# A fused chunked-attention and gated feed-forward kernel: SP's DMA queue in program order, 112-row first loads, feed-forward units moved ahead of an out-projection, masks by matmul

## The chip, the cores and the metric

The kernel runs on one core of one Trainium2 chip. The metric is the time of one execution on the device in microseconds (us). A *profile* is one execution recorded by the hardware profiler; its span runs from the first to the last recorded instruction and is about 1.7 us shorter than the time of the same execution (277.73 and 276.0 before); an execution's time also varies by a few us around the medians quoted. Engines are called as the profile calls them: PE (matmuls), PEld (its weight loads), DVE (vector), ACT (scalar), POOL (general), SP (here it only issues DMAs); "SPq" is SP's instruction queue. Each engine has one queue of instructions, and in these profiles one that waits holds up those behind it (below, a cast on DVE that waits 3.88 us). A scheduler decides the order of each queue when the kernel is built, from its own guess of durations. `keep_in_program_order` pins an instruction behind the one that the program writes before it for the same engine; where that one is not pinned and moves ahead, the pinned one can follow it (`e9_b2_after_wout` shows a case).

## The reference

Four batches of 768 tokens, 8 heads of 64. A chunk of 32 queries sees 16 keys to its left, itself, 8 keys to its right, and 8 memory keys. The result, 3072 tokens of 512 features, goes through a gated feed-forward layer.

```python
for c in range(nc):                                   # 24 chunks of 32
    k_full = concat([mem_k, k[:, :, max(0, 32*c-16) : min(S, 32*c+40)]])
    v_full = ...                                      # the same of v
    a = softmax(q_c @ k_full.T / 8)
    out[:, :, 32*c : 32*c+32] = a @ v_full
x = out.transpose(0, 2, 1, 3).reshape(3072, 512)
y = (relu(x @ w_gate) * (x @ w_val)) @ w_out          # 512 -> 1536 -> 512
```

## The kernel before

It works in 8 blocks of 384 tokens (half a batch). A block's feed-forward is 12 *dff units* (each four gate matmuls and four value matmuls of 128x384, then a product on DVE) and an *out-projection* (36 matmuls of 128x512, three stores). The attention of block n+1 is woven between the dff units of block n, so that in the long run PE never stops. I call "block n" the stage from the end of block n-1's out-projection to the end of its own.

Blocks 0 and 1 must be quick to start: four tokens per partition, so 100 partitions for 400 keys, and transposes on PE. The later blocks are loaded one token per partition, and keys, queries and attention output are transposed by DMAs issued from SP. SP thus issues three kinds of DMA in one queue: loads, transposes, and stores.

```python
KROWS = 100
def sp(dst, src):   return pin(nc.sync.dma_start(dst, src))      # pin = keep_in_program_order
def pool(dst, src): return pin(nc.gpsimd.dma_start(dst, src))

# start (cut): block 0 on SP and ACT, then weights on POOL, then block 1, then the rest
for h0 in (0, 4):
    b0.load_kv("k", h0, 4, sp); b0.load_q(h0, 4, act); b0.load_kv("v", h0, 4, sp)
# POOL waits until block 0's second keys are here, then loads w_gate, w_val columns 0 to 511
weights(0, 256); weights(256, 512)
sp(w_here[:, 0:1], w_val_sb[0:1, 0, 0:1])        # SP waits for the first weights
for h0 in (0, 4): ...                            # block 1's k, q, v, all on SP
# POOL waits until block 1's second keys are here, then
weights(512, 1024); weights(1024, 1536)
for c in range(0, NDC, 4): pool(w_out_sb[:, c:c + 4], ...)

# main loop (cut): ffn = 12 dff units, then the 3 units of the out-projection
    if n == 0:
        def first_load(b2=b2):
            sp(w_here[:, 1:2], w_out_sb[0:1, NDC - 1, 0:1])   # SP waits for w_out
            b2.load(sp)
        steps[11] = [first_load]
    elif n + 2 < NBLK:
        steps[0] = [lambda b2=b2: b2.load(nc.sync.dma_start)]   # not pinned
    ...                                          # steps 8 to 14: casts and transposes of block n+2

    def turn_k(self): nc.sync.dma_start_transpose(self.kT..., self.kn...)      # not pinned
    def turn_q(self): nc.sync.dma_start_transpose(self.qT..., self.qn...)      # not pinned
    def cast_q(self): ... nc.vector.tensor_copy(self.qn..., view...)
    def cast_v(self): nc.vector.tensor_copy(self.vb[:, :, :, 0:D], self.vf); ...
```

The softmax here doesn't subtract the row's maximum and nothing guards it: scores larger than these inputs give would overflow.

## Time and profile before

281.69 us (median of 2 runs, 281.11 to 282.26). The profiled span is 276.0 us. The page's head gives busy time by engine, and rows of 40 slices of 6.9 us each in tenths; PEclk is the granted PE clock, DMA the mean busy share of the 16 DMA engines.

```profile
span 276.0 us, 4450 instructions
PE 235.2 (85%) x1592; PEld 136.2 (49%) x1592; DVE 154.2 (56%) x399; ACT 112.1 (41%) x229; POOL 32.8 (12%) x60
PE   0386756994999989989989997959999999999994
PEclk9999595999799999999999999986999999999999
DMA  6698899959799798984997799398601121111001
```

The next view cuts the span into stretches: length, busy time of each engine (with the number of instructions), mean clock, DMA share, GB/s. The cuts are at the first gate matmul (29.6), the end of block 1's out-projection (108.0), and the ends of blocks 2 to 5.

```profile
0.00:29.60 29.60, 12.80 (x125) 9.65 (x126) 17.66 (x57) 15.53 (x33) 15.46 (x45) 0.97 0.79 170
29.60:108.00 78.40, 66.06 (x436) 37.33 (x436) 43.07 (x112) 30.56 (x65) 9.78 (x11) 0.90 0.97 188
108.00:135.10 27.10, 25.94 (x182) 15.19 (x181) 18.65 (x46) 11.56 (x23) 1.88 (x1) 1.00 0.91 193
135.10:162.80 27.70, 26.31 (x182) 15.02 (x181) 19.31 (x48) 11.56 (x23) 1.88 (x1) 1.00 0.90 176
162.80:197.10 34.30, 29.16 (x182) 15.78 (x181) 21.61 (x50) 11.56 (x23) 3.77 (x2) 0.90 0.91 185
197.10:222.80 25.70, 25.70 (x182) 15.24 (x181) 14.16 (x38) 11.56 (x23) 0.00 (x0) 1.00 0.16 48
```

Block 5 (the last row) has PE busy in all of its 25.7 us, and that is what a block costs when nothing disturbs it. Blocks 2, 3 and 4 take 27.1, 27.7 and 34.3: 12.0 us more than three such blocks. The first two blocks take 108.0 us.

The load of block 7's queries (178.29) stands behind a transpose of attention output, which can go only when that attention is done. It landed at 184.8. On DVE a cast of those queries stands in order between products that PE needs, and waits for them:

```profile
184.78 0.56 DVE L257 CAST qn_106<-qf 128x768 bf16<-128x768 f32 x1 [3.88 <-DMA qf<-in_q_dram]
```

On PE this is seen:

```profile
185.86 1.44 PE L360 MATMUL vl_ps<-xT,w_val_sb 128*128 128x384 f16 x4 [3.24 <-DVE gvT L365]
187.10 10.14 PE L375 MATMUL out_ps<-w_out_sb,gvT 128*128 128x512 f16 x36
```

PE waited 3.24 us, then ran at half its clock for a few microseconds: four value matmuls in 1.44 us (0.81 elsewhere), an out-projection in 10.14 (7.93 elsewhere).

### The profile page before, as it was taken

The numbers are of one execution on the slowest core, as the hardware profiler recorded it, in microseconds if no ns is written. First come the engines' busy times: TensorE is split into PE (matmuls) and PEld (weight loads), VectorE is DVE, ScalarE is ACT, GpSimd is POOL, SyncE is SP. The second block draws the span as 40 slices with busy tenths as digits, with TensorE's granted clock in tenths as the row PEclk, the third lists the DMA queues.
The fourth block names the chain that finished last, engine by engine and source line by source line (L and its number), as shares of the span: only waits on it lengthen the run. The fifth ranks groups of instructions, "written<-read, shape, count | busy, mean of one in ns | idle before, by whom it ended". The sixth has DMA issues, their size and how long they took to land.

```text
span 276.0 us, 4450 instructions
## 1 busy us (share of the span) xinstructions
PE 235.2 (85%) x1592; PEld 136.2 (49%) x1592; DVE 154.2 (56%) x399; ACT 112.1 (41%) x229; POOL 32.8 (12%) x60
## 2 busy tenths in 40 slices
PE   0386756994999989989989997959999999999994
PEld 0264322653455645655546554633566466645641
DVE  5566131586527973896289619944687138703410
ACT  1575522554435523642345234520365246414321
POOL 8490250000020200020020002000200000000000
PEclk9999595999799999999999999986999999999999
DMA  6698899959799798984997799398601121111001
GB/s 163 185 131 184 216 206 196 197 88 255 121 210 252 117 201 263 194 174 96 274 201 152 163 208 252 62 211 150 173 14 32 52 77 23 37 76 40 0 38 77
DMA packets 96506, 39.76 MB, mean 144 GB/s; under 512 B 76324, under 2 KB 93412, under 8 KB 96484
## 3 DMA queue, kind: packets, MB, share of 16 engines
q1 hardware_dynamic: 89620, 33.97, 56.9%
q0 software_dynamic: 5808, 4.72, 11.0%
q10 hardware_dynamic: 1056, 0.79, 1.0%
q8 instruction: 12, 0.20, 0.3%
q14 instruction: 10, 0.08, 0.1%
HBM read 30.03 MB, written 6.29 MB: 132 GB/s over the span
## 4 chain that ended last, share of the span: by engine, by line
PE 55%; DMA 20%; DVE 10%; issue 6%; POOL 4%; SPq 2%; ACT 1%; DVEq 0%; POOLq 0%; ACTq 0%
PE out_ps L375 23%; PE vl_ps L360 14%; PE g_ps L356 14%; DMA w_out_sb<-in_moe_w_out_dram 8%; DMA qf<-in_q_dram 4%; DVE gvT L365 4%; DMA kf_100<-in_k_dram 3%; DVE x_big L313 2%; DMA w_val_sb<-in_moe_w_val_dram 2%; PE s_ps L294 2%; DMA kf_99<-in_k_dram 2%; SPq L387 2%; DVE ex_111 L302 1%; PE o_ps L308 1%; POOL w_gate_sb L390 1%
## 5 line engine op out<-in xcount | busy, mean ns | idle before, releaser
L360 PE MATMUL vl_ps<-xT,w_val_sb 128*128 128x384 f16 x384 | 82.2, 337 | 6.6 <-DVE gvT L365 4.1
L356 PE MATMUL g_ps<-xT,w_gate_sb 128*128 128x384 f16 x384 | 81.8, 335 | 4.9 <-DMA w_gate_sb<-in_moe_w_gate_dram 3.4
L365 DVE TENSOR_TENSOR gvT<-vl_ps,g_relu 128x384 f16<-128x384 f32 x96 | 52.9, 552 | 56.3 <-PE vl_ps L360 55.4
L363 ACT ACTIVATE g_relu<-g_ps 128x384 f16<-128x384 f32 x96 | 47.1, 490 | 52.9 <-PE g_ps L356 38.4
L375 PE MATMUL out_ps<-w_out_sb,gvT 128*128 128x512 f16 x288 | 65.8, 388 | 0.0
L360 PEld LDWEIGHTS <-w_val_sb 128*128 128x128 f16 x384 | 38.3, 100 | 33.9 <-issue 8.3
L356 PEld LDWEIGHTS <-w_gate_sb 128*128 128x128 f16 x384 | 36.6, 100 | 24.0 <-issue 3.9
L375 PEld LDWEIGHTS <-gvT 128*128 128x128 f16 x288 | 28.7, 100 | 34.9 <-issue 3.3
L378 ACT COPY o_sb<-out_ps 128x512 f32<-128x512 f32 x24 | 14.0, 585 | 59.4 <-PE out_ps L375 59.4
L313 DVE TENSOR_TENSOR x_big<-o_ps,rinv 96x256 f16<-96x256 f32 x64 | 26.5, 414 | 0.8
L299 ACT ACTIVATE ex_110<-s_ps 128x384 f16<-128x384 f32 x22 | 10.9, 493 | 12.8 <-PE s_ps L294 8.8
L294 PE MATMUL s_ps<-qz_97,kb 128*128 128x192 bf16 x64 | 11.0, 257 | 3.9 <-DVE qz_97 L212 3.6
L294 PEld LDWEIGHTS <-kb 128*128 128x128 bf16 x128 | 10.2, 99 | 6.9 <-issue 3.9
L299 ACT ACTIVATE ex_112<-s_ps 128x384 f16<-128x384 f32 x21 | 10.3, 492 | 7.4 <-PE s_ps L294 5.7
L299 ACT ACTIVATE ex_111<-s_ps 128x384 f16<-128x384 f32 x21 | 10.3, 492 | 7.3 <-PE s_ps L294 6.9
L311 DVE RECIPROCAL rinv<-o_ps 96x4 f32<-96x4 f32 x64 | 10.8, 168 | 2.1 <-PE o_ps L308 2.0
L294 PE MATMUL s_ps<-qz_98,kb 128*128 128x192 bf16 x64 | 11.0, 244 | 0.0
L302 DVE TENSOR_TENSOR ex_111<-ex_111,mask_int 128x384 f16<-128x384 f16 x16 | 10.1, 630 | 0.2
L308 PEld LDWEIGHTS <-ex_111 128*128 128x128 f16 x84 | 5.0, 100 | 10.1 <-DVE ex_111 L302 6.6
L257 DVE CAST qn_106<-qf 128x768 bf16<-128x768 f32 x6 | 3.2, 551 | 11.0 <-DMA qf<-in_q_dram 11.0
L267 POOL CAST vb_108<-memv 8x2048 f16<-8x2048 f32 x2 | 3.8, 1883 | 44.8 <-DVE vb_108 L264 44.8
L267 POOL CAST vb_107<-memv 8x2048 f16<-8x2048 f32 x2 | 3.9, 1950 | 40.0 <-DVE vb_107 L264 40.0
(114 smaller groups left out, 184.4 us busy)
## 6 DMA issues: line engine op xcount, KB each, us to landing
out_dram<-o_sb SPq DMA_DIRECT2D x24, 256.0 KB
qf<-in_q_dram SPq DMA_DIRECT2D x6, 768.0 KB
vf_102<-in_v_dram SPq DMA_DIRECT2D x12, 240.0 KB
vf_101<-in_v_dram SPq DMA_DIRECT2D x12, 240.0 KB
kf_100<-in_k_dram SPq DMA_DIRECT2D x9, 256.0 KB
kf_99<-in_k_dram SPq DMA_DIRECT2D x9, 256.0 KB
w_out_sb<-in_moe_w_out_dram POOLq DMA_DIRECT2D x3, 512.0 KB, 20.4
w_gate_sb<-in_moe_w_gate_dram POOLq DMA_DIRECT2D x2, 512.0 KB, 10.3
```

Source lines behind the costliest of these rows:

```text
L294: nc.tensor.matmul(s_ps[:, i], lhsT=blk.kb[:, 2 * g + i, j, :], rhs=blk.qz[:, 2 * g + i, :, :, 32 * j:32 * j + 32], start=True, stop=True)
L299: nc.scalar.activation(e, s_ps.rearrange("p a x s c -> p (a x) (s c)"), ACT.Exp, scale=SCALE)
L302: nc.vector.tensor_tensor(out=e, in0=e, in1=m4, op=ALU.mult)
L308: nc.tensor.matmul(o_ps[:, i, :], lhsT=st["ex"][:, i, :], rhs=blk.vb[:, j, 4 * g + i, :], start=True, stop=True)
L311: nc.vector.reciprocal(rinv, o_ps[0:QB, :, D:D + 1])
L313: nc.vector.tensor_tensor(out=x_big[:, 256 * g:256 * g + 256].rearrange("p (h d) -> p h d", h=4), in0=o_ps[0:QB, :, 0:D], in1=rinv_b, op=A ...
L356: nc.tensor.matmul(g_ps, lhsT=w_gate_sb[:, f, 128 * m:128 * m + 128], rhs=blk.xT[:, f, :], start=(f == 0), stop=(f == NFC - 1))
L360: nc.tensor.matmul(vl_ps, lhsT=w_val_sb[:, f, 128 * m:128 * m + 128], rhs=blk.xT[:, f, :], start=(f == 0), stop=(f == NFC - 1))
L363: nc.scalar.activation(g_relu, g_ps, ACT.Relu)
L365: nc.vector.tensor_tensor(out=state["gvT"][:, m].rearrange("p t j c -> p j t c"), in0=vl_ps.rearrange("p (j t c) -> p j t c", j=NJ, t=NT), ...
L375: nc.tensor.matmul(out_ps, lhsT=state["gvT"][:, m, t].rearrange("p j c -> p (j c)"), rhs=w_out_sb[:, m, :], start=(m == 0), stop=(m == NDC ...
L378: nc.scalar.copy(o_sb, out_ps)
```

## The change

Its intents: SP's whole queue is pinned, so that loads go before the stores and transposes that follow them in the program; loads are given in the order of need, and each block's preparation is moved up; the first two blocks are loaded in 112 rows (of four tokens, so 448 tokens instead of 400), to use more DMA engines; block 1's dff units come before block 0's out-projection, so that `w_out` is needed later; the masks of blocks 0 and 1 are added to the scores by a small matmul instead of a product on DVE; in the later blocks the cast of q goes to ACT, that of v to POOL; and idle matmuls are put in at the start to keep the PE clock up. The core of the diff (the rest is renaming, the two halves of start attention handled four heads at a time, and the building of masks; further, in the start the cast of v moves from ACT to DVE and the memory keys and values of block 0 are loaded from ACT, and `gvT`, the dff units' product, gets a second buffer, since with the new order two blocks' products are kept at once):

```diff
-    KROWS = 100
+    KROWS = 112
-            nc.sync.dma_start_transpose(self.kT...)          # likewise qT, xT, and the stores
+            pin(nc.sync.dma_start_transpose(self.kT...))
-                nc.vector.tensor_copy(self.qn[...], view[:, x])
+                pin(nc.scalar.copy(self.qn[...], view[:, x]))
-            nc.vector.tensor_copy(self.vb[:, :, :, 0:D], self.vf)
+            pin(nc.gpsimd.tensor_copy(self.vb[:, :, :, 0:D], self.vf))
             # scores of blocks 0 and 1: mask added in PSUM before the exponential
+                if on_pe:
+                    nc.tensor.matmul(s_ps[:, i], lhsT=lows[kind], rhs=ids["chunks"], start=False, stop=True)
-            nc.vector.tensor_tensor(out=e, in0=e, in1=m4, op=ALU.mult)
+            if not on_pe:
+                ...                                          # as before
+    warm(8, 512)                                 # before the first attention; 4 more inside its second half
 # loads of the start, in program order (cut)
+    load_start(b0)                               # k, q, v of 4 heads, twice, on SP
+    pool_after(0, b0.kr[...]); weights(0, 512)
+    weights(512, 1024)
+    sp_after(0, w_gate_sb[0:1, 0, 512:513])      # SP waits for the weights 512 up, then block 1
+    load_start(b1)
+    pool_after(1, b1.kr[...]); weights(1024, 1536)
+    def second_loads():                          # during block 0's dff units
+        sp_after(1, w_gate_sb[0:1, 0, 1024:1025])
+        for f in b2.pieces(sp): f()
+        pool_after(2, b2.qf[...])                # w_out only after block 2's queries
+        for c in range(0, NDC, 4): pool(w_out_sb[:, c:c + 4], ...)
+    run(dff[0], hooks, [], [])
+    run(dff[1] + outs[0] + outs[1], hooks, att, ...)      # was dff0, outs0, dff1, outs1
 # later blocks
-            steps[0] = [lambda b2=b2: b2.load(nc.sync.dma_start)]
+            for i, f in enumerate(blocks[n + 2].pieces(sp)):   # one piece per unit, pinned
+                add(hooks, i, f)
-            # casts and transposes at units 8, 9, 10, 14
+            prepare(blocks[n + 2], (hooks, 7), (hooks, 8), (hooks, 10), (hooks, 12))
```

## The prediction

> **What bounds the kernel now.** The windows view splits the 276.0 us span at 29.6 us (first gate matmul), 108.0 (second out-projection done) and 248.5 (last block begins). Blocks 5 and 6, with almost no loads in flight (DMA share 0.16), take 25.7 us each with PE busy throughout: the PE floor of a block. Blocks 2, 3, 4 take 27.1, 27.7 and 34.3. The first two blocks take 108.0 us, against about 63 us of PE work at full clock (estimate: 2 x 23.4 dff and out-projection, 2 x 8 attention). So about 45 us are lost up front and 12 in blocks 2 to 4; the tail is 4 us.
>
> Causes, from PE timeline, waits and chain of waits:
> - Start: keys are usable at 7.3 us, the second values only near 19. DMA share is 0.63 in the first 10 us. The Trainium skill, "DMA: Bandwidth & Descriptors", section "Why a DMA increments its semaphore by 16 and not by 1", says 100 partitions spread over 10 engines; 10/16 = 0.63 agrees.
> - Weights for dff units 4 up wait behind block 1's loads (3.4 + 2.3 us of PE waits near 40), and w_out must land (59.6) before block 2's loads start: 8% of the chain.
> - After such waits four gate matmuls take 1.28 us instead of 0.65 for about 4 us (PEclk 0.66 to 0.77). The skill's "TensorE: Matmul & The Clock Gate", Part 1, says an idle window halves the clock; the trace agrees.
> - Block 4: a q load issued late (178.3, landed 184.8) holds the DVE cast, then 3.2 us PE wait and 10.1 us instead of 7.9 for the out-projection.
>
> **What the change does.**
> 1. 112-row loads use 16 engines: block 0's 2.6 MB at 174/0.63 = 276 GB/s, about 10 us, second values near 13 us. But DVE's order puts the second keys' cast before the first key copies, so first scores start near 13, as before. Mask multiplies leave DVE (16 x 0.35 us) for 32 small matmuls (2.7 us PE). First gate matmul near 25 (-5).
> 2. Loads in need order: weights 0 to 1023 right after block 0, then block 1, the rest, block 2, and w_out last, hidden by block 1's dff (15.6 us). PE still waits 2 to 4 us for weights 1024 up in block 1's attention. Warm-up matmuls save the half clock. Second out-projection ends near 91 (-17).
> 3. Loads go ahead of stores in SP's order, q cast moves to ACT (1.1 us per block), v cast to POOL (1.23 us on DVE; estimate 2 us there, from the 1.9 us mem_v casts). Blocks 2 to 6: 26.2 us each, 131 instead of 140.4 (-9). DMA has about 23.5 engine-share us of work per 27 us block: close to full, but should keep up.
> 4. Last block and tail unchanged, 27.5 us.
>
> Sum: 91 + 131 + 27.5 = 249.5 us of span, 26 to 27 less. Time: 253 us, range 244 to 264. Faster by over 2%: 0.96, within 0.03, slower 0.01.
>
> **What would show it.** DMA share near 1 in the first 10 us; second values cast by 14 us; first gate matmul 22 to 27; no weight wait over 4 us; second out-projection done 86 to 96; blocks 2 to 6 at 25.7 to 27 us with no DVE wait for q; mean PE clock above 0.97.
>
> **What would make it wrong.** DMA unable to feed 26 us blocks (waits for k or v in blocks 2 to 5); POOL's v cast slowed by, or slowing, DVE; PE's fixed order holding block 1's attention behind a dff matmul that waits for weights; a half clock that warm-up does not prevent. If DMA order gains more than I allow, the first two blocks could take as little as 80 us.

## More of the kernel before

How SP's order does harm shows in its issues. The first number is the start of the issue, the second its length; the length of a group (x3) includes the gaps between its members.

```profile
29.75 7.76 SPq L236 DMA_DIRECT2D kf_100<-in_k_dram  x3
37.70 0.48 SPq L237 DMA_DIRECT2D kf_100<-in_k_dram  x1
...
59.65 0.59 SPq L387 DMA_DIRECT2D w_here<-w_out_sb  x1
...
177.06 1.18 SPq L322 DMA_TRANSPOSE xT<-x_big  x1
178.29 0.59 SPq L167 DMA_DIRECT2D qf<-in_q_dram  x1
```

## The result and the profile after

253.43 us (median of 2 runs, 253.36 to 253.49). Executions over 1.5% slower than the fastest of the same kernel are left out of the means. A ratio here is the mean time of one kernel's fast runs over that of the other's fast runs of the same rounds, so not quite the ratio of the quoted medians; it is 0.900, with a 95% interval of 0.892 to 0.908. The same views of the kernel after, cut again at the first gate matmul, at the end of block 1's out-projection and at the ends of the blocks:

```profile
span 251.7 us, 4515 instructions
PE 229.7 (91%) x1636; PEld 138.0 (55%) x1636; DVE 137.4 (55%) x353; ACT 114.7 (46%) x221; POOL 47.6 (19%) x81
PE   6287899999799957999999999999999999999994
PEclk9559999999999999999999999999999999999999
DMA  6999999999897999896498949994989401130012
```

```profile
0.00:28.90 28.90, 17.55 (x152) 12.17 (x153) 14.48 (x41) 12.11 (x21) 20.35 (x61) 0.82 0.97 202
28.90:91.20 62.30, 59.96 (x452) 36.76 (x451) 35.92 (x87) 31.51 (x61) 12.24 (x12) 1.00 1.03 202
91.20:121.50 30.30, 25.84 (x180) 15.26 (x181) 18.70 (x48) 12.82 (x25) 5.61 (x3) 1.00 0.84 172
121.50:147.20 25.70, 25.70 (x181) 15.26 (x180) 15.82 (x43) 12.82 (x25) 1.89 (x1) 1.00 0.85 184
147.20:172.90 25.70, 25.70 (x181) 15.25 (x180) 16.92 (x43) 12.82 (x25) 5.61 (x3) 1.00 0.86 185
172.90:198.60 25.70, 25.70 (x182) 15.26 (x180) 15.82 (x43) 12.82 (x25) 1.89 (x1) 1.00 0.87 181
```

Blocks 3, 4 and 5 now stand at 25.7 us with PE always busy, and block 5 does so with loads in flight (DMA share 0.87). The slices of PEclk show a reduced clock only in the start (how far that row can be trusted there is said at the end). Two things are not what one would wish: the first gate matmul comes at 28.9, hardly sooner than the 29.6 of before, and block 2 takes 30.3 us. Its excess is in two waits on PE:

```profile
94.10 0.82 PE L409 MATMUL g_ps<-xT,w_gate_sb 128*128 128x384 f16 x4 [2.90 <-DMA xT<-x_big]
...
99.41 0.33 PE L343 MATMUL s_ps<-qz_98,kb 128*128 128x192 bf16 x2 [1.56 <-DVE qz_98 L332]
```

The first is a wait for the last transpose of block 2's attention output, which SP issued at 90.01, behind block 3's transpose of queries (88.45):

```profile
88.45 1.47 SPq L311 DMA_TRANSPOSE qT<-qn_106  x1
90.01 2.31 SPq L375 DMA_TRANSPOSE xT<-x_big  x1
```

DVE had finished that output at 86.9; an earlier transpose of attention output (86.24) and a store (87.83) stood before it as well. The second wait follows from the first: DVE's copies of block 3's keys and queries stand behind block 2's first product (95.69), which needs the late matmuls. In a second profile of this kernel (`e0_after`) the first wait is 2.8 us, the second only 0.2, but the first matmuls after the wait run at half the clock; block 2 takes 30.4 us there too.

The budget, from such cuts of the profiles (us). The middle column is the kernel before with nothing but SP's order pinned; it is an experiment of the next section.

| Stretch | before | before, SP pinned | after |
|---|---|---|---|
| to the first gate matmul | 29.6 | 28.4 | 28.9 |
| first two blocks' feed-forward, block 2's attention | 78.4 | 74.4 | 62.3 |
| blocks 2, 3, 4 | 27.1, 27.7, 34.3 | 25.7, 25.7, 25.7 | 30.3, 25.7, 25.7 |
| blocks 5, 6 | 25.7, 25.7 | 25.7, 25.7 | 25.7, 25.8 |
| block 7 and tail | 27.5 | 27.4 | 27.3 |
| span | 276.0 | 258.7 | 251.7 |

### The profile page after: what moved, and what is told of

The parts are those of the page before. It is cut to its first block, busy times and chain, and to the rows that moved or that the text cites. A ratio compares the mean times of both kernels' runs of the same rounds, so it can differ in the third digit from the quotient of the medians.

```text
span 251.7 us, 4515 instructions
## 1 busy us (share of the span) xinstructions
PE 229.7 (91%) x1636; PEld 138.0 (55%) x1636; DVE 137.4 (55%) x353; ACT 114.7 (46%) x221; POOL 47.6 (19%) x81
## 4 chain that ended last, share of the span: by engine, by line
PE 82%; DMA 7%; DVE 4%; ACT 3%; issue 2%; SPq 1%; DVEq 0%; ACTq 0%
PE vl_ps L413 24%; PE g_ps L409 24%; PE out_ps L428 23%; PE s_ps L343 4%; DMA qf<-in_q_dram 4%; PE o_ps L361 4%; PE v_ps L258 2%; DMA xT<-x_big 2%; DMA qT<-qn_105 2%; PE s_ps L347 1%; SPq L88 1%; DVE kb L238 1%; DVE gvT L418 1%; ACT vb_107 L261 0%; ACT o_sb L431 0%
## 5 line engine op out<-in xcount | busy, mean ns | idle before, releaser
L409 PE MATMUL g_ps<-xT,w_gate_sb 128*128 128x384 f16 x384 | 78.5, 326 | 3.3 <-DMA xT<-x_big 2.9
L413 PE MATMUL vl_ps<-xT,w_val_sb 128*128 128x384 f16 x384 | 78.6, 326 | 0.0
L428 PE MATMUL out_ps<-w_out_sb,gvT 128*128 128x512 f16 x288 | 64.0, 379 | 0.0
L413 PEld LDWEIGHTS <-w_val_sb 128*128 128x128 f16 x384 | 37.3, 98 | 24.2
L409 PEld LDWEIGHTS <-w_gate_sb 128*128 128x128 f16 x384 | 36.0, 98 | 21.9 <-DMA xT<-x_big 3.4
L428 PEld LDWEIGHTS <-gvT 128*128 128x128 f16 x288 | 28.1, 98 | 32.1
L366 DVE TENSOR_TENSOR x_big<-o_ps,rinv 96x256 f16<-96x256 f32 x64 | 26.6, 418 | 1.6
L343 PE MATMUL s_ps<-qz_97,kb 128*128 128x192 bf16 x64 | 11.8, 255 | 4.3 <-DVE qz_97 L251 2.5
L343 PE MATMUL s_ps<-qz_98,kb 128*128 128x192 bf16 x64 | 11.0, 244 | 1.6 <-DVE qz_98 L332 1.6
L280 POOL COPY vf_101<-memv 8x2048 f32<-8x2048 f32 x3 | 5.7, 1886 | 26.4 <-DMA memv<-in_mem_v_dram 18.2
L258 PE MATMUL v_ps<-vc,sel_171 114*128 114x256 f16 x32 | 5.4, 317 | 3.6 <-DVE vc L222 3.6
L325 DVE COPY kb<-kT 128x1440 bf16<-128x1440 bf16 x6 | 4.5, 758 | 5.9 <-DMA kT<-kn_104 3.0
L361 PEld LDWEIGHTS <-ex_110 128*128 128x128 f16 x88 | 5.7, 100 | 3.1 <-ACT ex_110 L351 0.4
L361 PEld LDWEIGHTS <-ex_111 128*128 128x128 f16 x84 | 5.2, 98 | 3.1 <-ACT ex_111 L351 0.8
```

The lines of the kernel that those rows point to most:

```text
L258: nc.tensor.matmul(ps[:, i], lhsT=sels[self.T][:, s, j + i], rhs=self.vc[:, 4 * h:4 * h + 4, D * s:D * s + D], start=(s == 0), stop=(s == ...
L343: nc.tensor.matmul(s_ps[:, i], lhsT=blk.kb[:, 2 * g + i, j, :], rhs=blk.qz[:, 2 * g + i, :, :, 32 * j:32 * j + 32], start=True, stop=not o ...
L361: nc.tensor.matmul(o_ps[:, i, :], lhsT=st["ex"][:, i, :], rhs=blk.vb[:, j, 4 * g + i, :], start=True, stop=True)
L366: nc.vector.tensor_tensor(out=x_big[:, 256 * g:256 * g + 256].rearrange("p (h d) -> p h d", h=4), in0=o_ps[0:QB, :, 0:D], in1=rinv_b, op=A ...
L409: nc.tensor.matmul(g_ps, lhsT=w_gate_sb[:, f, 128 * m:128 * m + 128], rhs=blk.xT[:, f, :], start=(f == 0), stop=(f == NFC - 1))
L413: nc.tensor.matmul(vl_ps, lhsT=w_val_sb[:, f, 128 * m:128 * m + 128], rhs=blk.xT[:, f, :], start=(f == 0), stop=(f == NFC - 1))
```

## The experiments

Twelve kernels ran, all with correct results. They fell into four groups, each on one chip with its own runs of the kernel before (medians here are of all of these runs; the ratios leave the slow ones out): the first group (the edits of 100 rows, masks, warm-up, out-projection first) had it at a median of 278.84 us, the second (repeat of the changed kernel, free SP, casts, late weights) at 280.03, the third (late block 2 loads, pinned before, `c3_both`) at 280.01, the fourth (`c4_turn_first`) at 280.33. Across groups I compare ratios, and take differences under about 1% as unresolved. Landmarks come from one profile each. Two profiles of the changed kernel itself differ by about 1 us at the landmarks (first gate matmul 28.9 and 29.8; span 251.7 and 252.3).

My theory at this point: the gain is that of the data's order, on SP and between SP and POOL. The rivals: that it comes from the new start (112 rows, masks, warm clock), from the reordered feed-forward alone, or from work moved off DVE.

### The changed kernel again (e0_after)

No edit; it is the base for the second group, and for the rest.

> The changed kernel itself again, as the control of this batch and of the one before: 252 to 256 us, ratio to the kernel before 0.90 to 0.92. All theories expect the same.

253.58 us (four fast runs, 252.9 to 256.65), ratio 0.9092 (0.902 to 0.917). Differences below are from this, unless the first profile is named.

### 100 rows (e1_rows100)

```diff
-    KROWS = 112
+    KROWS = 100
```

> The changed kernel with 100 rows per start load instead of 112, nothing else. Theory A (the width of the loads matters because 100 rows use 10 DMA engines): DMA share of the first 10 us falls from 0.83 to about 0.63, the second values of block 0 land some 3 us later, first gate matmul 31 to 33 us instead of 28.9, time +2 to +6 us. Rival B (the start is bound by the order of casts on ACT and DVE, not by load width): time within 1 us of the changed kernel.

Two of four runs are left out; the fast ones took 255.3 and 257.2 us, ratio 0.923 (0.912 to 0.934). The first gate matmul came at 31.7 (29.8 in the repeat, 28.9 in the first profile), the second out-projection ended at 93.2 (91.9 and 91.2), span 253.6. The first row is of this kernel, the second of the changed one:

```profile
0.00:10.00 10.00, 4.78 (x22) 2.09 (x23) 3.95 (x12) 2.11 (x2) 5.98 (x23) 0.89 0.64 165
```

```profile
0.00:10.00 10.00, 4.65 (x22) 2.12 (x23) 4.38 (x12) 2.11 (x2) 6.45 (x23) 0.87 0.83 219
```

DMA share 0.64 against 0.83, 165 GB/s against 219: the rows do what they are meant to. What arrives at the first gate matmul is 2 to 3 us, what arrives at the end 1 to 2 in the span, and 3.8 by the ratios, with only two runs.

### Masks on DVE again (e2_mask_dve)

```diff
-        kind, on_pe = kind_of(NJ * blk.T + j), blk.n < NSTART
+        kind, on_pe = kind_of(NJ * blk.T + j), False
```
(and the DVE masks of the first blocks built early instead of the matmul's operands)

> The changed kernel with the masks of blocks 0 and 1 multiplied on DVE again, no mask matmuls. Theory A (the DVE multiplies lie on the start's chain, 16 x 0.35 us): first gate matmul about 1 to 2 us later, time +1 to +3 us. Rival B (PE saves 2.7 us of mask matmuls and DVE has slack): time 0 to 2 us shorter.

254.44 us (253.26 to 255.13), ratio 0.916 (0.909 to 0.922). The second out-projection ended at 93.9, 2.0 us later than in the repeat, but the span was 253.4, 1.1 longer: part of it was given back in block 2. It is 0.9 us by the medians and 1.8 by the ratios: not resolved.

### No warm-up matmuls (e3_no_warm)

```diff
-        for _ in range(n):
+        for _ in range(0):
```

> The changed kernel without its 12 warm-up matmuls. Theory A (the 8 early ones are useless, since PE is idle again from 8.3 to 12 us and the clock is 0.61 in 10 to 20 us anyway; the 4 late ones keep the clock up at the first gate matmul): first dff units at half clock for up to 4 us, time +0.5 to +2.5 us. Rival B (attention keeps PE busy enough on its own): within 0.5 us.

253.96 us (253.22 to 255.84), ratio 0.916 (0.908 to 0.923): nothing that can be told from the changed kernel. The first gate matmul came earlier, at 27.7, but at half the clock. The first lines of the dff units without the warm-up:

```profile
27.67 0.94 PE L409 MATMUL g_ps<-xT,w_gate_sb 128*128 128x384 f16 x4 [0.57 <-ACT xT L380]
28.41 1.49 PE L413 MATMUL vl_ps<-xT,w_val_sb 128*128 128x384 f16 x4
```

Block 0's dff units were done at 56.1, against 55.8 and 56.7. So the four late fillers delay the first gate matmul by about a microsecond and save about as much clock. The eight early ones do nothing that lasts. Without them eight key transposes take 0.94 us; with them 0.57 in the first profile and in the repeat, but 0.94 again in six of the nine other kernels of this section that have them, so not even this is surely theirs. PE then sits 3.6 us for values in either kernel, and the first score matmul starts at 14.11 without and 14.25 with them, at the low clock in both (0.36 us a matmul; 0.24 later).

### Block 0's out-projection first (e4_out_first)

```diff
-    run(dff[1] + outs[0] + outs[1], hooks, att, ...)
+    run(outs[0] + dff[1] + outs[1], hooks, att, ...)
```

> The changed kernel with block 0's out-projection put back ahead of block 1's dff units, loads unchanged. Theory A (dff of block 1 hides the landing of w_out, issued only after 51 us): PE waits 8 to 12 us for w_out near 54 us, followed by a half clock; time +8 to +13 us. Rival B (DMA as a whole bounds the first 90 us, so PE's order only moves the wait): time less than +3 us.

258.07 us (256.88 to 259.83), ratio 0.928 (0.920 to 0.936): 4.5 us more than the repeat by the medians, the most among the parts of the new start that were tested:

```profile
60.27 9.83 PE L428 MATMUL out_ps<-w_out_sb,gvT 128*128 128x512 f16 x36 [3.31 <-DMA w_out_sb<-in_moe_w_out_dram]
```

PE waits 3.31 us for `w_out`, and the clock falls for the matmuls after it: 36 of them in 9.83 us instead of 7.93. Together that is 5.2 us, which is the loss up to a microsecond. I had expected a wait of 8 to 12 us.

### SP's later queue not pinned (e6_sp_free)

```diff
-            pin(nc.sync.dma_start_transpose(...))          # kT, qT, xT, stores, and the loads from block 3 on
+            nc.sync.dma_start_transpose(...)
```

> The changed kernel with the loads, transposes and stores of blocks 2 to 7 on SP left to the scheduler again (the program text is unchanged; the loads of blocks 3, 5, 7 then sink between the stores, and the next block's small loads float up). Theory A (program order on SP is what keeps blocks 3 to 6 at the floor of 25.7 us): late q or k loads return, at least two of the blocks 2 to 6 take over 27 us, time +3 to +12 us. Rival B (with loads already started two blocks ahead, order on SP does not matter): every one of blocks 3 to 6 within 0.5 us of 25.7, time within 1.5 us of the changed kernel.

One of four runs was slow; the three fast ones 256.95 to 259.42, ratio 0.924 (0.916 to 0.931). The blocks from 2 to 6 took 31.8, 26.5, 26.1, 25.7 and 25.7 us, the second out-projection ended at 92.4. The pins that this edit removes are worth about 4 us in the changed kernel. Neither theory holds whole: the loss is that of A, but no block after block 2 passes 27 us. These 4 us are far from what I had blamed on SP's order in the kernel before, and they called for the mirror experiment, the pinned kernel before, below.

### The casts on DVE again (e7_casts_dve)

```diff
-                pin(nc.scalar.copy(self.qn[...], view[:, x]))
+                pin(nc.vector.tensor_copy(self.qn[...], view[:, x]))
-            pin(nc.gpsimd.tensor_copy(self.vb[...], self.vf))
+            pin(nc.vector.tensor_copy(self.vb[...], self.vf))
```

> The changed kernel with the q and v casts of blocks 2 to 7 put back on DVE (2.3 us per block). Theory A (a cast that waits for its load stalls DVE and with it PE, as in block 4 of the kernel before): one or more blocks longer than 26.5 us, time +1.5 to +8 us. Rival B (loads now land well before their casts, and DVE is only about half busy): time within 1 us.

Two slow runs of four; the fast ones 254.45 and 256.44, ratio 0.914 (0.905 to 0.923), which the repeat's interval holds. Blocks 3 to 6 took 25.7 us each, so DVE has room for these casts in the steady blocks; block 2 took 32.1. Not resolved, at most about 2 us.

### Weights 512 to 1023 after block 1's loads (e8_weights_late)

```diff
-    weights(512, 1024)
-    sp_after(0, w_gate_sb[0:1, 0, 512:513])
+    sp_after(0, w_gate_sb[0:1, 0, 0:1])
 ...                                              # block 1's loads and the gate on its keys
+    weights(512, 1024)
```

> The changed kernel with weight columns 512 to 1023 loaded after block 1's keys again, as before the change. Theory A (need order of weights is worth the 5.7 us of PE waits near 40 us and a half clock of the kernel before): PE waits 2 to 6 us for weights between 33 and 42 us, dff of block 0 ends 59 to 63 us instead of 55.8, time +3 to +7 us. Rival B (the total of bytes bounds this stage, block 1's loads arriving earlier gives it back): less than +1.5 us.

255.19 us (254.49 to 256.5), ratio 0.912 (0.906 to 0.918), not separable from the repeat by time alone. In the profile, block 0's dff units end at 60.4 instead of 55.8 in the first profile of the changed kernel (first gate matmul at 28.9 in both; 56.7 in the repeat), with waits of 1.8 and 0.8 us for weights. The second out-projection ends at 94.5 instead of 91.2 (91.9 in the repeat). The direction is shown by the waits, which the changed kernel doesn't have; the size in time is not.

### Block 2's loads after `w_out` (e9_b2_after_wout)

```diff
-        sp_after(1, w_gate_sb[0:1, 0, 1024:1025])
-        for f in b2.pieces(sp): f()
-        pool_after(2, b2.qf[0:KROWS, 0, 0:1])
         for c in range(0, NDC, 4): pool(w_out_sb[:, c:c + 4], ...)
+        sp_after(1, w_out_sb[0:1, NDC - 1, 0:1])
+        for f in b2.pieces(sp): f()
```

> The changed kernel with w_out loaded ahead of block 2's inputs again, which then start only when w_out has landed, as before the change. Theory A (block 2's loads have to run before w_out, because block 2's attention is due in the middle of block 1's stage): block 2's keys and queries land about 10 us later, its first scores near 75 us instead of 69, PE waits 4 to 9 us between 66 and 80 us and again for later parts, second out-projection done at 96 to 102 us instead of 91 to 92, time +4 to +10 us. Rival B (there is slack, and the stage is bounded by PE): less than +2 us.

259.58 us (258.31 to 260.19), ratio 0.929 (0.923 to 0.934), 6 us lost, but not where I looked for it. I meant to make block 2's attention late. It wasn't: the wait of the scores for queries was 0.4 us. Instead PE waited 5.0 us in block 0's dff units, for weights 1024 up:

```profile
PE g_ps L409 <- DMA w_gate_sb<-in_moe_w_gate_dram: 5.0, 1, 5.0
```

The edit also took away the gate that held `w_out` back. Its issue on POOL was still pinned, but behind instructions that were not, and POOL issued it at 29.5 us, ahead of the last gate and value weights (34.8), which the program writes earlier. So `w_out` was on the DMA engines when those weights came, and shared the engines with them. The Trainium skill, "DMA: Bandwidth & Descriptors", section "Issuing engines are not separate DMA queues", says that DMAs of all issuing engines run on the same 16 DMA engines and interleave; this wait of 5.0 us agrees. The experiment is confounded for its own question, what late loads of block 2 cost. What it shows instead is the worth of holding `w_out` back until other data is here.

### The kernel before, with SP pinned and nothing else (e10_before_pinned)

```diff
-            nc.sync.dma_start_transpose(...)               # kT, qT, xT
+            tc.keep_in_program_order(nc.sync.dma_start_transpose(...))
-                nc.sync.dma_start(out[...], o_sb)
+                tc.keep_in_program_order(nc.sync.dma_start(out[...], o_sb))
-            steps[0] = [lambda b2=b2: b2.load(nc.sync.dma_start)]
+            steps[0] = [lambda b2=b2: b2.load(sp)]
```

> The kernel before with one part of the change alone: all its SP transfers in program order, nothing else. Theory A (the order on SP is what made block 4 take 34.3 us, since its q load was issued late behind stores and transposes): blocks 2 to 4 take 25.7 to 27.5 us each instead of 27.1, 27.7 and 34.3, the first 108 us are unchanged, time -5 to -11 us against the kernel before. Rival B (the transfers themselves are the bound there, total DMA share 0.9): blocks 2 to 4 together still above 86 us, time within 3 us of the kernel before.

260.06 us (259.15 to 262.16), ratio 0.932 (0.926 to 0.938). One pinned queue in the kernel *before* gives 20 of the 26.5 us that the changed kernel gains in the medians of these groups (280.0 to 253.6). Its blocks 4 and 5 (blocks 2 and 3 take 25.7 us as well):

```profile
154.20:179.90 25.70, 25.70 (x182) 15.23 (x180) 17.83 (x46) 11.58 (x23) 1.88 (x1) 1.00 0.87 184
179.90:205.60 25.70, 25.70 (x182) 15.26 (x180) 18.42 (x46) 11.58 (x23) 1.88 (x1) 1.00 0.95 185
```

These blocks have the q and v casts on DVE, no pieces, and the late preparation, and run at the floor. The last row, block 5, has a DMA share of 0.95; in the kernel before it was 0.16, because there the scheduler had drawn block 7's loads and casts, which the program gives to block 5, forward into block 4, where they ran into one another. It also shortened the stage before them, where I had not looked for an effect of SP's order. The gate on `w_out` and block 3's first keys in its queue:

```profile
53.47 0.59 SPq L387 DMA_DIRECT2D w_here<-w_out_sb  x1
...
78.54 3.56 SPq L387 DMA_DIRECT2D kf<-in_k_dram  x4
```

In the kernel before, the two lines of SP at 29.75 and 37.70 that I passed over are these same loads: block 3's keys and one piece of its values, 1.06 MB (3 x 256, 32, 16 and 240 KB), which the scheduler had lifted over everything that waits. They went out as soon as block 1's casts (of keys on DVE, 26.5 to 37.7) had freed the buffers, and the transpose of those keys is issued only at 91.1. They were issued from 29.75 on, just ahead of the weights (issued from 32.9) for which PE then waited 3.4 and 2.3 us. Pinned, they are issued at 78.5, the waits for weights are 1.4 and 1.7 us, `w_out` lands at 53.5 instead of 59.7, and block 0's dff units take 38.0 us from the first gate matmul instead of 42.9. The waits for the gate weights, before and pinned:

```profile
PE g_ps L356 <- DMA w_gate_sb<-in_moe_w_gate_dram: 3.4, 1, 3.4
```

```profile
PE g_ps L356 <- DMA w_gate_sb<-in_moe_w_gate_dram: 1.4, 1, 1.4
```

The weights are 2.6 of these 4.9 us. Another 1.7 are one wait of PE, 3.1 us before (to 67.8) and 1.5 pinned (to 61.7), for masked scores that stand on DVE behind the cast of block 2's keys. Up to 29 us the two profiles have the same order on every engine, yet the pinned one is 1.2 us ahead at the first gate matmul: that is variation between runs, not a gain. From about 61 us on DVE's and PE's orders differ too, since the scheduler arranged them anew. So what is measured is the pins with all that follows from them.

### Two attempts to repair what was left (c3_both, c4_turn_first)

What was left: the late first gate matmul, and block 2's 4.6 us. In `c3_both` the start's casts are put in the order of need (second values and queries after the first half's copies), and block 2 is prepared some units earlier, with its attention moved up.

```diff
-    start_half(b0, att0, 0)
+    first_half(b0, att0)                 # second q cast and v cast pinned behind the first half's units
-    prepare(b2, (hooks, 1), (hooks, 2), (hooks, 4), (hooks, 6))
+    prepare(b2, (hooks0, 10), (hooks0, 11), (hooks, 4), (hooks, 4))    # in block 0's dff units
-    run(dff[1] + outs[0] + outs[1], hooks, att, [(8 + i, 10 + i - i // 7) for i in range(8)])
+    run(dff[1] + outs[0] + outs[1], hooks, att, [(6 + i, 8 + i) for i in range(8)])
```

> An attempt to beat the changed kernel: block 0's second-half casts are pinned behind the first half's copies on DVE and ACT, and the casts, transposes and scores of blocks 2 and 3 are moved one to two units ahead. Theory A (the first scores wait from about 9.7 to 14.3 us only because the second half's q cast stands ahead on ACT; and 2.9 us of PE wait at 91 us are the last xT transpose behind block 3's qT on SP): first scores near 10 us, first gate matmul 24 to 26 us instead of 28.9 to 29.8, no xT wait above 1 us, block 2 about 26 us instead of 30, time -4 to -8 us against the changed kernel. Rival B (the start is bound by the landing of the second half and later by the weights): first gate matmul moves by less than 1.5 us or the gain is lost in weight waits near 40 us; time -2 to -4 us, from block 2 alone.

254.33 us (252.22 to 255.0), ratio 0.909 (0.902 to 0.917): the same as the changed kernel. The first repair did its local work: first scores at 10.6 instead of 14.3, first gate matmul at 27.3. A new wait took the gain: 4.9 us of PE for block 2's queries, and the second out-projection ended at 94.3 instead of 91.2. Block 2 took 26.6 us, but this is no repair: its last attention output was transposed at 90.65 (90.01 in the changed kernel), again behind block 3's queries (89.08), and PE did not wait for it because block 2's dff units were due 3 us later. The transposes of block 2 were issued 6.4 us (keys) and 3.0 us (queries) earlier than in the changed kernel, and the queries landed only 1 us earlier (66.8 instead of 67.8):

```profile
54.48 6.34 SPq L313 DMA_TRANSPOSE kT<-kn  x1
60.93 3.50 SPq L322 DMA_TRANSPOSE qT<-qn  x1
```

The DMA engines were already as busy as they get there. Their share between 50 and 60 us is 1.26 in the changed kernel and 1.15 in this one (the share adds up the time that packets took, so it can exceed 1). In that traffic the issue of the keys' transpose itself took 6.34 us, against 2.91 for the later one.

In `c4_turn_first` I meant to get out of the traffic: block 2's keys and queries are cast on POOL as soon as they land and transposed at once, ahead of its values.

```diff
-        for f in b2.pieces(sp): f()
-        pool_after(2, b2.qf[0:KROWS, 0, 0:1])
+        pieces = b2.pieces(sp)
+        for f in pieces[:3]: f()             # keys, queries
+        b2.cast_kq_on_pool(); b2.turn_k(); b2.turn_q()
+        for f in pieces[3:]: f()             # values
```
(on top of `c3_both`)

> A second attempt to beat the changed kernel, built on c3_both: block 2's k and q are cast on POOL as soon as they land, their two transposes go on SP ahead of block 2's four v loads, and w_out is issued only after those casts. Theory A (in c3_both the transposes of block 2 stood behind v loads and beside w_out on full DMA engines, so issuing them 6 us earlier landed them only 1 us earlier): qT lands near 58 us instead of 66.8, no PE wait above 1.5 us between 54 and 80 us, second out-projection done near 87 to 90 us, span 245 to 248 us, time -3 to -7 us against the changed kernel (250 or less; ratio to the kernel before 0.88 to 0.895). Rival B (the DMA work due by then is the bound, whatever its order): the wait moves to v, w_out or block 3, second out-projection still 91 to 95 us, time within 1.5 us of the changed kernel.

258.7 us (six runs, 257.39 to 260.16), ratio 0.931 (0.924 to 0.937): worse. The transposes were issued at 49.2 and 52.7, but POOL issued `w_out` from 52.1, and the queries landed only at 66.3. The values behind them were issued only from 57.1 and landed at 73.6, and PE now waited for both:

```profile
PE o_ps L381 <- POOL vb L335: 4.2, 1, 4.2
PE s_ps L363 <- DVE qz L352: 4.0, 1, 4.0
```

No version that I tried beats the changed kernel clear of the noise.

## Why the prediction was right or wrong

The total was right: 253.0 us foretold, 253.43 measured, and the span's sum 249.5 against 251.7. Two landmarks were close as well, the second out-projection (91 foretold, 91.2 measured) and block 7 with its tail (27.5, 27.3). Not all the steps to them were.

**Step 1, the start: wrong.** "First gate matmul near 25 (-5)"; it came at 28.9, 0.7 us sooner than before. The 112 rows do what step 1 says of the engines: DMA share 0.83 in the first 10 us, 0.64 with 100 rows (I had looked for near 1). The Trainium skill, "DMA: Bandwidth & Descriptors", section "Why a DMA increments its semaphore by 16 and not by 1", lets a DMA be split over the largest number up to 16 that divides the outer dimension of both its sides, 10 for 100 rows and 16 for 112; the ratio 0.64/0.83 = 0.77 shows the direction, and that the mean of that window is not wholly in these loads. The data came, and was not used at once: the second values were cast at 14.2 ("near 13" was foretold), and it took another 14.7 us to the first gate matmul. These are DVE's and ACT's instructions at that time in the changed kernel:

```profile
10.64 0.69 DVE L220 CAST kn_103<-kf_99 114x1024 bf16<-114x1024 f32 x1 [4.46 <-DMA kf_99<-in_k_dram]
11.25 0.69 DVE L222 CAST vc<-vf_101 114x1024 f16<-114x1024 f32 x1
11.85 0.96 DVE L238 COPY kb<-k_ps 128x360 bf16<-128x360 bf16 x2
```

```profile
12.08 0.83 ACT L220 CAST qn_105<-qf 128x768 bf16<-128x768 f32 x1 [4.61 <-DMA qf<-in_q_dram]
12.82 0.79 ACT L250 COPY qz_97<-q_ps 64x768 bf16<-64x768 bf16 x1
```

The casts for the *second* half of the heads (10.64, 12.08) stand in front of the copies that the *first* half needs (11.85, 12.82). I had seen that on DVE and put it in step 1, "first scores start near 13, as before", but not on ACT, where the queue held it for as long. `c3_both`, which puts those casts in the order of need, has its first scores at 10.6 and its first gate matmul at 27.3. So the order is a cause, but not the whole: 3.7 us won at the first scores became 1.6 at the first gate matmul, and 2 us to my 25 remain. The term that I had too small is what lies between: from the first scores (13) to the first gate matmul (25) I gave 12 us, for which I had no working. It takes 14.7 us in the changed kernel, 16.6 in the kernel before and 16.7 in `c3_both`. No load is in it: in the changed kernel the chain of waits has its last DMA at 12.1 us and then goes to and fro between PE, ACT and DVE. My 19 us for the second values before was misread likewise: at 19.0 ACT casts them without having waited for a load. The low clock may be part of it: 128x192 matmuls stay at 0.36 or 0.37 us until about 17 us in the changed kernel and 16 in `c3_both`, where they begin 3.7 us sooner. How much it costs was not tested.

**Step 2, loads in need order: right, with two terms that cancel.** I allowed 2 to 4 us of waiting for the weights from 1024 up. The first of them landed at 39.9, PE uses them from 41.8, and there is no such wait. From the first gate matmul to the second out-projection I had 66 us (25 to 91); it took 62.3. The 4 us too few there and the 4 us too many of step 1 are the reason that 91 was hit. The order's parts, one at a time: the out-projection behind block 1's dff units about 4.5 us; 112 rows 1 to 4 us; weights 512 up before block 1, shown in waits, 1 to 3 us; warm-up and masks 2 us or less each, unresolved. "Warm-up matmuls save the half clock" is right of the four late ones, and they cost about what they save; it was wrong of the eight early ones.

**Step 3, the later blocks: right in its gain, wrong in where it is.** 131 us for blocks 2 to 6 foretold, 133.2 measured, 7.3 less than before. I spread 0.5 us over each block; instead four stand at 25.7 or 25.8, and block 2 takes 30.3, for the two waits shown above. There, as the profile reads, SP's program order works against the kernel: block 2's last attention output stands behind a transpose for block 3. No run exchanges these two, so this is read and not shown. The named worry, that DMA could not feed 26 us blocks, did not come true at shares of 0.84 to 0.87.

**What I did not see at all: what SP's order had cost in the first two blocks.** I gave its gain to step 3 alone (the late queries of block 4) and read the first two blocks as weights waiting behind block 1's loads. They waited behind block 3's too. `e10_before_pinned` shows that pinning SP, in a kernel otherwise unchanged, takes 12.0 us off blocks 2 to 4 and 5.2 off what comes before (108.0 to 102.8; 1.2 of them are the variation named above), 17.3 of the 24.3 us of span with the tail. The whole rest of the change, all the new start, weights, order and casts, brings the first two blocks from 102.8 to 91.2 and gives 4.6 back in block 2.

**The parts do not add.** Taking the later pins out of the changed kernel costs about 4 us (`e6_sp_free`); putting them into the kernel before gains 20. With loads cut into pieces, given at units of the program and with gates on POOL, the scheduler has less to lift in the changed kernel; its blocks 3 and 4 take 26.5 and 26.1 us without the pins, not 27.7 and 34.3. I take this to be the reason; which of pieces, gates or earlier preparation does it was not tested. So it makes no sense to say that a given part of the change gives a given share. A part's worth depends on which others are there.

What stays open: whether block 2 could be freed without delay elsewhere. `c3_both` and `c4_turn_first` say that between 40 and 70 us the loads they moved forward moved others back. The mean DMA share from first gate matmul to second out-projection is 1.03, with PE busy in 59.96 of 62.3 us, so there is little left to gain on either there. In the start PE is busy in only 17.6 of 28.9 us, so there is more to gain there; `c3_both` won 1.6 us of it and lost them again later.

## What to carry to other kernels

Where loads, transposes and stores share one in-order queue and a scheduler is free to arrange it, look first at what stands ahead of what in the queue, from its beginning. A load that is issued too early, because its buffer happens to be free, can do harm as well as one too late, and it shows nowhere as a wait of its own, only as waits for other data; pin the order and try this alone before rebuilding anything. When a repair makes one transfer earlier while the DMA engines are full, expect another to be later, as in `c3_both` and `c4_turn_first`, and ask beforehand which one can afford it.

## What the Trainium skill lacked or had wrong

- "TensorE: Matmul & The Clock Gate", Part 1, has the throttled clock as the state at the beginning, and warns that the trace's clock events are unreliable. Both are borne out, in a form that it does not name: in several runs the clock row reads 1.00 from the beginning though PE is slow. Without the warm-up it reads 1.00 from 0 to 20 us, while eight key transposes take 0.94 us (0.57 in the first profile of the changed kernel) and a mask matmul 0.36 (0.24 later); in `c3_both`, which has the warm-up, it reads 1.00 as well, with the same 0.94 and 0.37. In the start, durations are the evidence, not the row.
- "GPSIMD Engine Reference", section 4.1, "Engine selection", calls a one-input operation on POOL "roughly line-rate", and the page has no time for one. Here a 128x2048 cast from f32 to f16 took 1.89 us on POOL and 1.23 on DVE. A copy of 8x2048 took 1.89 us too, so few partitions saved nothing.
- "DMA: Bandwidth & Descriptors", section "DMA Transpose (X-bar)", gives no time for the issue of a transpose on SP (elsewhere the page has cycles of the sequencer, in a comparison for trn3). Here the same transpose of keys took between 1.88 and 3.02 us to issue in the changed kernel, and 6.34 in the middle of other traffic (`c3_both`); the transpose of queries behind it was issued only when it was through, at 60.93.
